# First four heads of a fused attention and mixer kernel: the scores made a second time with the keys on the partitions

## The chip, the cores and the metric

The kernel runs on one core of a Trainium2 chip. The metric is the device time of one execution in microseconds (us); the time of the kernel before is the median of three runs.

The core's engines run beside each other, each with its own queue of instructions, and wait for each other by semaphores. TensorE (PE) multiplies and writes to PSUM; VectorE (DVE) and ScalarE (ACT) read and write PSUM and SBUF; GpSimd (POOL) works on SBUF; SyncE (SP) issues the DMA transfers.

## The reference

```
scores = (q @ k^T) / 8, positions of later blocks of 64 masked      # per batch (8) and head (8), 576 x 576
attn   = exp(scores - max(scores)); attn /= sum(attn) + 1e-9
x      = attn @ v, heads side by side                               # (8, 576, 512)
theta  = x @ w_theta
y      = w_tok_r @ (x cos theta) + w_tok_i @ (x sin theta)          # over the 576 positions
u      = x + y
out    = u + max(u @ w_ch, 0)
```

q, k and v are standard normal times 0.1, q and k times some 5.8 on top. All is f32. A position sees its own block of 64 and all earlier blocks.

## The kernel before

The work goes by batch (8) and, within a batch, by pairs of heads (4). A pair's two heads (hh = 0, 1) lie on the two halves of the 128 partitions, so products of 64 rows for both run beside each other. Positions are cut into four tiles of 128 queries (i = 0 to 3, positions 64 to 575) and a tile 4, the first 64 positions of both heads in one.

For a pair, `scores_wide` (tiles 3 and 2) and `scores_narrow` (tiles 1 and 0) make q k^T with the queries on the partitions (line 610), and `mask` (line 617) adds a huge negative number to the forbidden blocks. For a head, `maxima` (line 658, VectorE) takes the maximum of each row, `bias` (lines 668 and 670) turns it into the bias of the exponential, and `exponentials` (line 674, ScalarE) writes exp to SBUF (`t`). The products with v need the keys on the partitions, so exp has to be turned. For the first eight heads TensorE turns it (`turn_up`, line 699, in 128x128 f32 tiles into PSUM) and ScalarE or VectorE copies it to SBUF (`turned_high`, lines 451 and 453); for later heads a DMA turns it. For heads 0 to 3 (`WIDE_HEADS`) all stays f32 and `weighted` (line 732) multiplies with the raw v, which has a column of ones for the sum of the row. Later heads work with pairs of f16 numbers. `normalise` divides.

In batches 0 to 2 scores use the raw f32 q and k. The weights come as wide numbers and are unpacked in steps (`Weight`: load, exponent, lowest, narrow, plain, high and low part); this fills the first 60 us of ScalarE, VectorE and GpSimd. The mixer of a batch then has theta (line 898), sines, their products with x, the mixing over positions (line 974), and the channel products (line 997).

The order of the work is written out. `add` names each part, what it needs, which PSUM banks it takes and gives back, and on which engines it may run. `ORDER` lists the 3453 parts in the order in which they are issued, `BANKS` the PSUM banks, `PLACES` the engine of each part that has a choice. So each engine's queue follows from three tables. Sixteen parts `fill` (line 1270) are two products of ones each, whose results nobody reads.

Of the kernel before, what the change touches and what calls it, by code (L numbers as in the profile page):

```python
# [12 lines left out]
F32 = mybir.dt.float32  # L13
# [21 lines left out]
HALVED = 8  # L35
# [222 lines left out]
def attention_phase_mixer(  # L258
# [40 lines left out]
    def pieces(n):  # L299
        return ("A", "B") if n < 2 * HALVED else ("all",)  # L300
# [1022 lines left out]
```

## Time and profile before

| | |
|---|---|
| median of 3 runs | 641.83 us (641.12 to 641.84) |
| the profiled execution's own time | 642.9 us |
| its span, first to last instruction | 641.1 us |
| TensorE busy | 624.5 us, 97% |
| VectorE busy | 565.0 us, 88% |
| ScalarE busy | 525.0 us, 82% |
| GpSimd busy | 349.5 us, 55% |
| mean granted TensorE clock | 0.995 |

The span is one execution, as the profiler saw it. Busy time is the time in which an engine had an instruction in work. A TensorE instruction's duration is longer than the distance to the next one, since products follow each other in a pipeline; the cost of products is therefore read from start to start, as the timeline gives it. The granted clock is the share of 2.4 GHz that TensorE got.

### The profile page before, as it was taken

The page shows a single profiled execution, that of the slowest core. Times are in us where ns is not written, and L with a number is a line of the kernel's source. Part 1 is how long each engine was busy: PE and PEld are TensorE (multiplying, and loading weights), DVE is VectorE, ACT ScalarE, POOL GpSimd, SP SyncE. Part 2 cuts the span into 40 slices and gives each one's busy share as a digit, 9 for nine tenths or more (in the row PEclk, how much of TensorE's full clock was granted, in tenths as well). Part 3 has the DMA queues.
Part 4 walks back from the last instruction along what each step waited for, and adds up shares of the span by engine and source line. Part 5 has one row for each costly group of instructions (what it writes and reads, how often), then busy time and mean ns, then how long its engine had stood idle before and what let it go on. Part 6 is the DMA issues. An engine that isn't in the chain of part 4 may idle for free.

```text
span 641.1 us, 18144 instructions
## 1 busy us (share of the span) xinstructions
PE 624.5 (97%) x7457; PEld 469.1 (73%) x7457; DVE 565.0 (88%) x1111; ACT 525.0 (82%) x886; POOL 349.5 (55%) x387
## 2 busy tenths in 40 slices
PE   7999999999999999999999999999998999999997
PEld 4788667766876688867778678775876678857775
DVE  4999999999999999999999999999999998855564
ACT  5989999889897999989998999899998987346012
POOL 4545557523626654545775567672565478744230
PEclk9899999999999999999999999999999999999999
DMA  8973998998797799977869978969797757930102
GB/s 327 384 263 86 200 214 181 190 181 194 185 237 162 157 136 223 176 172 202 172 166 219 224 138 184 218 142 229 160 200 147 124 76 154 167 74 2 38 38 75
DMA packets 238627, 109.28 MB, mean 170 GB/s; under 512 B 225360, under 2 KB 226384, under 8 KB 238544
## 3 DMA queue, kind: packets, MB, share of 16 engines
q1 hardware_dynamic: 238544, 108.12, 76.3%
q8 instruction: 58, 0.95, 0.6%
q14 instruction: 25, 0.20, 0.1%
HBM read 42.21 MB, written 9.44 MB: 81 GB/s over the span
## 4 chain that ended last, share of the span: by engine, by line
PE 51%; ACT 16%; DVE 8%; DMA 7%; issue 3%; POOL 1%; POOLq 0%; DVEq 0%; ACTq 0%
PE g L974 12%; PE s L974 9%; PE g L997 7%; PE g L741 7%; DMA pt<-p 7%; ACT t L674 5%; PE s L997 4%; PE g L898 4%; PE s L898 3%; PE s L610 3%; ACT aa L941 2%; DVE p L456 2%; DVE m L658 2%; ACT rr L939 2%; ACT junk L860 2%
## 5 line engine op out<-in xcount | busy, mean ns | idle before, releaser
L974 PEld LDWEIGHTS <-zh 128*128 128x128 f16 x1152 | 112.7, 98 | 29.7 <-issue 0.4
L974 PE MATMUL g<-wT_h,zh 128*128 128x288 f16 x351 | 100.5, 286 | 0.8 <-ACT t L674 0.8
L974 PE MATMUL g<-wT_h,zl 128*128 128x288 f16 x351 | 100.4, 286 | 0.0
L974 PE MATMUL g<-wT_l,zh 128*128 128x288 f16 x351 | 100.4, 286 | 0.0
L741 PEld LDWEIGHTS <-pt 128*128 128x128 f16 x2700 | 89.1, 98 | 7.8 <-DMA pt<-p 3.2
L741 PE MATMUL g<-v,pt 128*128 128x65 f16 x2700 | 92.6, 193 | 2.1 <-DMA pt<-p 1.6
L658 DVE TENSOR_REDUCE m<-s 128x1 f32<-128x576 f32 (+3 forms) x132 | 84.9, 671 | 2.8 <-PE s L617 2.5
L456 POOL TENSOR_TENSOR p<-t,p 128x1536 f16<-128x1536 f32 (+4 forms) x22 | 55.8, 2542 | 50.5 <-ACT p L451 35.4
L456 DVE TENSOR_TENSOR p<-t,p 128x1600 f16<-128x1600 f32 (+4 forms) x42 | 72.1, 1717 | 4.9 <-ACT p L451 4.5
L451 ACT CAST p<-t 128x1536 f16<-128x1536 f32 (+4 forms) x50 | 68.1, 1363 | 3.4 <-DMA pt<-p 2.7
L974 PEld LDWEIGHTS <-zl 128*128 128x128 f16 x576 | 56.4, 98 | 15.8 <-issue 1.2
L898 PEld LDWEIGHTS <-xT 128*128 128x128 f16 x384 | 36.6, 98 | 42.6 <-issue 1.7
L974 PE MATMUL s<-wT_h,zh 128*128 128x288 f16 x225 | 64.3, 286 | 0.0
L974 PE MATMUL s<-wT_l,zh 128*128 128x288 f16 x225 | 64.3, 286 | 0.0
L974 PE MATMUL s<-wT_h,zl 128*128 128x288 f16 x225 | 64.3, 286 | 0.0
L674 ACT ACTIVATE t<-s,m,size 128x576 f32<-128x576 f32 (+1 forms) x80 | 59.7, 779 | 4.1 <-POOL m L670 2.4
L950 POOL TENSOR_TENSOR aa<-aa,xn 128x256 f32<-128x256 f32 (+1 forms) x59 | 42.3, 728 | 35.0 <-ACT aa L941 25.9
L658 DVE TENSOR_REDUCE m<-g 128x1 f32<-128x192 f32 (+2 forms) x156 | 53.8, 369 | 6.8 <-PE g L617 6.7
L997 PEld LDWEIGHTS <-wch_h 128*128 128x128 f16 x512 | 48.3, 98 | 13.4 <-issue 1.7
L456 POOL TENSOR_TENSOR xp<-xn,xp 128x640 f16<-128x640 f32 x22 | 33.6, 1529 | 33.5 <-ACT xp L451 24.8
L674 ACT ACTIVATE t<-g,m,size 128x320 f32<-128x320 f32 (+2 forms) x100 | 50.1, 534 | 1.3 <-POOL m L670 1.0
L997 PE MATMUL g<-uh,wch_h 128*128 128x288 f16 x176 | 50.4, 286 | 0.2 <-DVE xT L1013 0.2
(209 smaller groups left out, 1659.3 us busy)
## 6 DMA issues: line engine op xcount, KB each, us to landing
rv<-in_v SPq DMA_DIRECT2D x16, 780.0 KB, 5.9
rq<-in_q SPq DMA_DIRECT2D x15, 640.0 KB, 5.2
rk<-in_k SPq DMA_DIRECT2D x15, 576.0 KB, 4.8
out<-xT SPq DMA_DIRECT2D x28, 288.0 KB, 2.8
w_raw<-in_w_tok SPq DMA_DIRECT2D x5, 576.0 KB, 8.4
pt<-in_w_tok SPq DMA_DIRECT2D x4, 576.0 KB, 9.2
w_raw<-in_w_theta SPq DMA_DIRECT2D x4, 512.0 KB, 8.1
w_raw<-in_w_ch SPq DMA_DIRECT2D x4, 512.0 KB, 5.8
```

What stands on the lines that cost most here:

```text
L451: nc.scalar.copy(out=out, in_=x)
L456: engine_of(on).tensor_tensor(out=out, in0=x, in1=y, op=ALU.subtract)
L610: nc.tensor.matmul(to[hh][:, col:col + n], lhsT=qq[rows, P + P * i:P + P * i + P], rhs=kk[rows, k0:k0 + n], start=nn == 0 and col % 512 == ...
L658: nc.vector.tensor_reduce(out=self.m[:, i:i + 1], in_=self.scores_of(i), axis=AX.X, op=ALU.max)
L674: nc.scalar.activation(out=t_parts[self.hh][:, to:to + n], in_=self.scores_of(i), func=AF.Exp, scale=self.scales()[0], bias=self.m[:, NI + ...
L741: nc.tensor.matmul(o[:, i, :], lhsT=source[:, block, :], rhs=vv[:, slot, hh, :], start=first, stop=last)
L860: nc.scalar.activation(out=to, in_=x, func=AF.Abs, accum_out=self.scales_of(what, g).sum_of(what, g))
L898: nc.tensor.matmul(g, lhsT=xT[:, xx + i, :], rhs=ww[:, dt, :], start=first, stop=last)
L939: nc.scalar.activation(out=to, in_=x, func=AF.Sin, scale=2.0 * math.pi)
L950: engine_of(on).tensor_tensor(out=cd, in0=cd, in1=self.xns[dt][:, i0:i0 + ni, :], op=ALU.mult)
L974: nc.tensor.matmul(g, lhsT=zz[:, kk, cols], rhs=ww[:, kk, ts], start=(n == 0 and kk == k0 and nn == 0), stop=n == 4 and kk == k0 + ni - 1 ...
L997: nc.tensor.matmul(g[:, 0:HS], lhsT=ww[:, dt, e * P:(e + 1) * P], rhs=uu[:, dt, th * HS:(th + 1) * HS], start=dt == 0 and n == 0, stop=dt ...
```

## The change

For heads 0 to 3 exponentials, turns and copies are replaced. The scores with the queries on the partitions are made as before, but for their maxima alone. The maximum of each row is split into three bf16 parts (`less_upper`, two subtractions for a head). A product with a bf16 identity turns the parts of all tiles into 15 rows (`maxima_turned`), which a copy takes to SBUF (`maxima_row`). Then `scores_turned` makes the scores with keys and queries exchanged, in three banks for each head (sx, sy, sz): f32 products over full blocks, half blocks of 64 output rows in the bank sz, a bf16 product for the mask of the diagonal blocks, and bf16 products of a prepared matrix of minus ones with the rows of the maxima, which subtract the maximum of each query. `first_turned` does it for the first 64 positions. ScalarE's exponential goes from there into the tile that `weighted` reads (`exponentials_turned`), in the order of `TURNED_BLOCKS`; a head's products with v are one part now where they were two. The bias steps of these heads go. The identity, the minus ones and the rows lie in the room of `p_parts[1]`, which is used by later heads only, and are prepared at the start by VectorE and GpSimd.

The three tables are new as a whole: 3441 parts, in another order throughout. The 16 fills remain. On SP's queue the loads of pair 1's q and k stand behind three weight tiles where they stood behind four. In TensorE's queue the beginning is now:

```
before: s2.0 s1.0 sd.0 tp.1.B tp.0.B s2.1 tp.0.A fill tp.1.A fill wa.0 tp.0.4 wa.1 sd.1 wa.2 wa.3 s1.1 fill vm.0 weighted.0.A ...
after:  s2.0 s1.0 sd.0 s2.1 sd.1 fill mt.0 fill mt.1 s4.0 sx.0 sy.0 sz.0 fill wa.0 wa.1 wa.2 wa.3 s1.1 weighted.0 fill mt.3 wa.4 mt.2 fill vm.0 s4.1 sx.1 sz.1 wa.5 weighted.1 sy.1 ...
```

Here s1, s2 and sd are the scores of a pair, tp the turns of a head, wa a sum over weights, mt the turn of a head's maxima, and s4, sx, sy and sz the second scores of a pair. The core of the diff, without the tables:

```diff
+    TURNED_BLOCKS = [[(0, 1), (10, 0)], [(1, 1), (4, 2), (10, 5)], [(2, 1), (5, 2), (8, 3), (11, 0)],
+                     [(3, 1), (6, 2), (9, 3), (7, 4), (11, 5)], [(12, 0)]]
+    FULL = {"sx": [(1, 0, 4, 0)], "sy": [(2, 1, 3, 0), (4, 3, 1, 384)], "sz": [(3, 2, 2, 0)]}
+    HALF = {"sx": [], "sy": [], "sz": [(0, 0, 256), (1, 1, 256), (2, 0, 384), (3, 1, 384)]}
+    DIAGONAL = {"sx": [0], "sy": [0, 384], "sz": [0]}
+    MOST = {"sx": [0, 1, 2, 3], "sy": [1, 2, 3, 3], "sz": [2, 3, 5, 6]}
...
+    early = p_parts[1].rearrange("p a c -> p (a c)").bitcast(BF16)
+    ident_b = early[:, 0:P]
+    nc.vector.tensor_copy(out=ident_b, in_=made_ident)
+    one_of = const.tile([P, NI], F32, name="one_of")
+    for row in (0, 64):
+        nc.vector.tensor_reduce(out=one_of[row:row + 64], in_=ident[row:row + 64, row:row + 3 * NI].rearrange("p (s i) -> p i s", i=NI),
+                                axis=AX.X, op=ALU.add)
+    minus = early[:, P:P * (NI + 3)].rearrange("p (a c) -> p a c", c=P)
+    nc.vector.tensor_scalar(out=minus[:, 0:NI], in0=one_of.unsqueeze(2).broadcast_to([P, NI, P]), scalar1=-1.0, scalar2=None, op0=ALU.mult)
+    for i in range(2):
+        nc.gpsimd.tensor_copy(out=minus[:, NI + i, 0:D], in_=minus[:, 2 * i, 0:D])
+        nc.gpsimd.tensor_copy(out=minus[:, NI + i, D:P], in_=minus[:, 2 * i + 1, 0:D])
+    m_split = [const.tile([P, 3, NI], F32, name=f"m3{n}") for n in range(4)]
+    m_rows = [early[:, P * (NI + 3 + n):P * (NI + 4 + n)] for n in range(2)]
+    for part in m_split + m_rows:
+        nc.gpsimd.memset(part, 0.0)
...
+        def scores_turned(self, x):
+            qq, kk = self.raw("q"), self.raw("k")
+            to = [bank_of[x, self.p, hh] for hh in range(2)]
+            both = [(hh, slice(hh * D, hh * D + D)) for hh in range(2)]
+            for slot, i, n, col in FULL[x]:
+                for hh, rows in both:
+                    nc.tensor.matmul(to[hh][:, col:col + n * P], lhsT=kk[rows, P * slot - D:P * slot + D], rhs=qq[rows, P + P * i:P + P * (i + n)],
+                                     start=col == 0, stop=False, tile_position=(hh * D, 0))
+            for i, half, col in HALF[x]:
+                for hh, rows in both:
+                    nc.tensor.matmul(to[hh][half * D:half * D + D, col:col + P], lhsT=kk[rows, 0:D], rhs=qq[rows, P + P * i:P + P * i + P],
+                                     start=False, stop=False, tile_position=(hh * D, half * D))
+            for col in DIAGONAL[x]:
+                for hh, rows in both:
+                    nc.tensor.matmul(to[hh][D:P, col:col + D], lhsT=ones[rows, 0:D], rhs=mask_q[rows, 0:D], start=False, stop=False,
+                                     tile_position=(hh * D, D))
+            for n, i in enumerate(MOST[x]):
+                for hh, rows in both:
+                    nc.tensor.matmul(to[hh][:, n * P:n * P + P], lhsT=minus[rows, i, :], rhs=m_rows[self.p % 2][rows], start=False, stop=n == 3,
+                                     tile_position=(hh * D, 0))
+
+        def first_turned(self):
+            to = bank_of["t4", 2 * self.p][0:D, 0:P]
+            nc.tensor.matmul(to, lhsT=self.raw("k")[:, 0:D], rhs=self.raw("q")[:, 0:P], start=True, stop=False)
+            nc.tensor.matmul(to, lhsT=minus[0:D, NI - 1, 0:D], rhs=m_rows[self.p % 2][0:D], start=False, stop=True, tile_position=(0, 0))
...
+        def less_upper(self, step, on):
+            x = m_split[self.n % 4]
+            less(on, x[:, step + 1, :], x[:, step, :], self.uppers()[:, step * NI:step * NI + NI])
+
+        def maxima_turned(self):
+            to = bank_of["sx", self.pair.p, self.hh][self.hh * D:self.hh * D + 3 * NI, 0:P]
+            nc.tensor.matmul(to, lhsT=self.uppers(), rhs=ident_b, start=True, stop=True)
+
+        def maxima_row(self, on):
+            rows = slice(self.hh * D, self.hh * D + 3 * NI)
+            copied(on, m_rows[self.pair.p % 2][rows], bank_of["sx", self.pair.p, self.hh][rows, 0:P])
+
+        def exponentials_turned(self, x):
+            if x == "t4":
+                to, src, rows = wide_of(self.turned)[0:D, 12, :], bank_of[x, self.n][0:D, 0:P], slice(0, D)
+            else:
+                at_ = 4 * ("sx", "sy", "sz").index(x)
+                to, rows = wide_of(self.turned)[:, at_:at_ + 4, :], slice(0, P)
+                src = bank_of[x, self.pair.p, self.hh].rearrange("p (a c) -> p a c", c=P)
+            nc.scalar.activation(out=to, in_=src, func=AF.Exp, scale=QK_SCALE, bias=lift[rows, 0:1])
...
+                if turned_early:
+                    for step in range(2):
+                        add(("ms", n, step), step_of(h.less_upper, step), [("ms", n, 0)] if step else [("m", n, i) for i in tiles], on="PD")
+                    add(("mt", n), h.maxima_turned, [("ms", n, 1)], takes=[("sx", p, hh)])
+                    add(("mc", n), h.maxima_row, [("mt", n)] + row_free, on="DA")
+                    for x in ("sx", "sy", "sz") + ("t4",) * (hh == 0):
+                        add(("ex", n, x), step_of(h.exponentials_turned, x), [("s4" if x == "t4" else x, p)] + w_free,
+                            leaves=[(x, n) if x == "t4" else (x, p, hh)])
+                    add(("weighted", n, piece), step_of(h.weighted, piece), turned_of(n, piece) + turned_of(heads[0], piece) + [("vo", pr // PG)] + o_free)
+                    continue
```

## Rows read from the trace of the kernel before

**Rows 1.** The page, part 1: busy us, share, instructions of each engine.
```profile
PE 624.5 (97%) x7457; PEld 469.1 (73%) x7457; DVE 565.0 (88%) x1111; ACT 525.0 (82%) x886; POOL 349.5 (55%) x387
```

**Rows 2.** Windows: length, busy us of each engine (instructions), clock, DMA share, GB/s.
```profile
13.60:98.30 84.70, 82.94 (x866) 62.34 (x866) 79.17 (x179) 79.57 (x145) 47.13 (x61) 0.96 0.83 235
103.40:530.00 426.60, 419.63 (x5435) 314.17 (x5432) 404.73 (x785) 391.68 (x646) 243.20 (x239) 1.00 0.87 178
530.00:641.10 111.10, 107.26 (x1036) 82.96 (x1031) 69.23 (x126) 42.26 (x75) 50.54 (x49) 1.00 0.33 76
```

**Rows 3.** Waits of TensorE: who waited for whom, us in total, times, longest.
```profile
PE g L699 <- ACT t L674: 1.9, 1, 1.9
...
PE g L610 <- DMA rq<-in_q: 1.1, 1, 1.1
...
PE g L638 <- ACT t L674: 1.0, 2, 0.8
```

**Rows 4.** Windows of 1 us at the start; the number behind POOL is the granted clock.
```profile
12.00:13.00 1.00, 0.56 (x6) 0.32 (x3) 1.00 (x4) 1.00 (x3) 0.91 (x2) 0.92 1.04 423
13.00:14.00 1.00, 0.36 (x2) 0.39 (x4) 1.00 (x2) 1.00 (x3) 0.59 (x1) 0.50 1.04 427
...
19.00:20.00 1.00, 1.00 (x8) 0.99 (x7) 0.79 (x3) 1.00 (x2) 0.00 (x0) 0.66 0.97 399
```

**Rows 5.** Windows, with the fills' line alone, over the whole span.
```profile
0.00:641.10 641.10, 9.18 (x32) 2.88 (x32) 0.99 0.77 170
```

**Rows 6.** Timeline of TensorE, turns: start, us, line, operands, count [idle before].
```profile
18.48 1.63 PE L699 MATMUL s<-ident_r,t 128*128 128x128 f32 x8
...
57.11 1.04 PE L699 MATMUL s<-ident_r,t 128*128 128x128 f32 x8
57.98 1.52 PE L741 MATMUL g<-v,pt 128*128 128x65 f16 x45
```

**Rows 7.** Timeline of TensorE, 39.2 to 41.5 us: a pair's wide scores and mask.
```profile
39.25 2.17 PE L610 MATMUL s<-rk,rq 64*128 64x512 f32 x16
41.25 0.22 PE L617 MATMUL s<-ones,mask_q 64*128 64x128 bf16 x2
41.40 0.77 PE L699 MATMUL g<-ident_r,t 128*128 128x128 f32 x5
```

**Rows 8.** Timeline of TensorE, theta's last rows in two column halves.
```profile
85.34 0.41 PE L901 MATMUL g<-wth_h,xT 128*64 128x256 f16 x4
85.59 0.28 PE L901 MATMUL g<-wth_l,xT 128*64 128x256 f16 x2
```

**Rows 9.** Timeline of TensorE, narrow f16 scores of a later pair, and its mask.
```profile
309.64 0.84 PE L610 MATMUL g<-qk 64*128 64x320 f16 x18
310.31 0.22 PE L617 MATMUL g<-ones,mask_q 64*128 64x128 bf16 x2
```

**Rows 10.** Groups, 0 to 43.3 us: line, operation, shapes, count, busy us, mean ns, idle before.
```profile
L674 ACT ACTIVATE t<-s,m 128x576 f32<-128x576 f32 (+1 forms) x8 | 5.3, 696 | 0.4 <-POOL m L670 0.4
...
L674 ACT ACTIVATE t<-g,m 128x320 f32<-128x320 f32 (+2 forms) x12 | 4.8, 441 | 0.1
...
L453 DVE COPY pt<-s 128x1024 f32<-128x1024 f32 (+1 forms) x3 | 2.6, 905 | 0.4 <-ACT junk L860 0.4
...
L451 ACT COPY pt<-s 128x1024 f32<-128x1024 f32 x2 | 2.0, 1004 | 0.0
...
L451 ACT COPY pt<-g 128x512 f32<-128x512 f32 (+1 forms) x3 | 1.4, 478 | 0.0
L453 DVE COPY pt<-g 128x512 f32<-128x512 f32 x2 | 1.4, 680 | 0.0
...
L497 ACT ACTIVATE w_raw<-w_raw,eighth 128x576 int32<-128x576 uint8 x1 | 0.8, 835 | 0.0
...
L501 DVE TENSOR_SCALAR w_raw<-w_raw 128x576 uint32<-128x576 uint32 x1 | 0.5, 453 | 0.0
```

**Rows 11.** Timeline of VectorE, its first maxima and the wait before them.
```profile
7.21 0.89 DVE L658 TENSOR_REDUCE m<-g 128x1 f32<-128x320 f32 x2 [4.74 <-PE g L617]
```

More of the change, by code (lines that the diff above doesn't have):

```diff
@@ L223 @@
+    "1235401235401235401234601235401234601234601234501235401235601235601234601235601236501234601236401236501236524654"
+    "0651445650546624654130143066645166605051431066645545056616026345051046561046656405340414405544416542015464160645"
+    "5646464100451345323640256314365612053040412045362400310266664645546"
 )
 PLACES = (
[L225 to L226 removed]
@@ new lines @@
+    "PAPASADAPADDAPADAPADAPADAAAAPDAPPPADDDPDADAAADAAADDPAADDADAAPDDAAPAPASAAAPADDADADDAPDPAADAAPADAAAAAPADASPAPDAAAP"
+    "ADPAAPDPDAADPDADADAAPAAAADAADAAAADAAAAAAADDSPAPDSAAAPADAAPAPDDAAPPDDDAPPPAAAAAPADAAPDDDPAAADADDSDAPDPAAAPDPASDAD"
+    "DPAAAAAPDAAAPAPPPADDDAAAADAAPPAPAPAPDAADDPDAPDPAPDPPPDDDDDPPDPDADDDAPDPAPDPAPPPDPPADPPADAAAAADDAAADAPDPAPDDDADDD"
+    "PPDPAPDDPPPDAPDPADDPADPPADPPDDPPADPPADDADADDPAAAAAADAAPDPDAPPPAAADADDADPDAPDPPPPPPPPDAPDPAPDDAPPDAPPPPDPPAPPDDAP"
+    "PPAAAAADDADAPADPPADDDDADPPAPDPAPDPAPDPPPPPAPDPAPDPAPDPAPPDADPPADPPDADPPADAAAAADDAPPPADAPAAAAAPPAPDPPPDPAPPDADPPP"
@@ L235 @@
+    "PPPAPPPAPDPAPDDAPDPADPAPAPPPADDAADAADADADPDAPDADDDPPPDDPAPDPADPPAPDDADPPAPPPADDDAPPDPPPPPPDDDAPADAAAADDAAAADAPAP"
+    "PDDDDDAPDPDDPPPPPAPPDAPPPPDPPDPDPDDPDAPPPPDPDPPPDDDPADPAAAAAAADADADPPADDDDADPDDDPDADDPAPDDPDDDADPPPDDPDPDPDDDPAD"
+    "DPDDPAPAPDPPAAADADAA"
 )
@@ L299, in pieces @@
     def pieces(n):
-        return ("A", "B") if n < 2 * HALVED else ("all",)
+        return ("A", "B") if WIDE_HEADS <= n < 2 * HALVED else ("all",)
     def extent(hh, piece):
@@ L656, in maxima, with uppers @@
             if not hasattr(self, "m"):
-                self.m = at.tile([P, 10], F32, tag="m", name="m", bufs=4)
+                self.m = m_split[self.n % 4][:, 0, :] if self.n < WIDE_HEADS else at.tile([P, 10], F32, tag="m", name="m", bufs=4)
             nc.vector.tensor_reduce(out=self.m[:, i:i + 1], in_=self.scores_of(i), axis=AX.X, op=ALU.max)
+        def uppers(self):
+            return m_split[self.n % 4].rearrange("p a c -> p (a c)").bitcast(BF16).rearrange("p (c two) -> p c two", two=2)[:, :, 1]
+        def less_upper(self, step, on):
[15 more added lines that the diff above has]
+            nc.scalar.activation(out=to, in_=src, func=AF.Exp, scale=QK_SCALE, bias=lift[rows, 0:1])
         def scales(self):
@@ L705, in turned_parts @@
             x = self.turned_in(piece)[:, 0:n * P].rearrange("p (a c) -> p a c", c=P)
-            if self.n < WIDE_HEADS:
-                at_ = {"A": 4, "B": 0, "4": 12}[piece]
-                return x, wide_of(self.turned)[:, at_:at_ + n, :], None
             return (x,) + tuple(self.turned[:, at_ + y:at_ + y + n, :] for y in (0, room // P))
@@ L730, in weighted @@
                 if self.n < WIDE_HEADS:
+                    blocks, rows = TURNED_BLOCKS[i], slice(0, P if i < 4 else D)
                     for j, (at_, slot) in enumerate(blocks):
-                        nc.tensor.matmul(o[:, i, :], lhsT=wide_of(source)[:, at_, :], rhs=pair.raw("v")[:, slot, hh, :],
+                        nc.tensor.matmul(o[:, i, :], lhsT=wide_of(source)[rows, at_, :], rhs=pair.raw("v")[rows, slot, hh, :],
                                          start=j == 0, stop=j == len(blocks) - 1)
@@ L1081, in attention_phase_mixer @@
     mixers = [Mixer(b) for b in range(B)]
+    again = ["sx", "sy", "sz", "s4"]
     for b, m in enumerate(mixers):
@@ L1088, in attention_phase_mixer @@
                         for n in ({"q": ["ql"], "k": ["kl"], "v": ["v2"]} if b >= WHOLE else
-                                  {"q": ["s1", "s2", "sd"], "k": ["s1", "s2", "sd"], "v": ["v2"]})[what] if what != "v" or 2 * p >= WIDE_HEADS]
+                                  {"q": ["s1", "s2", "sd"] + again * (2 * p < WIDE_HEADS), "k": ["s1", "s2", "sd"] + again * (2 * p < WIDE_HEADS), "v": ["v2"]})[what] if what != "v" or 2 * p >= WIDE_HEADS]
                 if what == "v":
@@ L1123, in keys, with early_done @@
         return [(name, n, x) for x in pieces(n)]
+    def early_done(n):
+        return [(x, p) for p in range(WIDE_HEADS // 2) for x in again] if n == WIDE_HEADS + 1 else []
     for p in range(B * NPAIR):
@@ L1145, in attention_phase_mixer @@
         add(("s2", p), pair.scores_narrow, ready, takes=[("s2", p, hh) for hh in range(2)])
-        add(("sd", p), pair.scores_first, ready + turn_of("first", [("e", heads[0], 4)], 2))
+        add(("sd", p), pair.scores_first, ready + turn_of("first", [("me"[heads[0] >= WIDE_HEADS], heads[0], 4)], 2))
+        if 2 * p < WIDE_HEADS:
+            row_free = turn_of("m_row", [(x, p) for x in again], 2)
+            known = [("mc", n) for n in heads]
+            for x in again:
+                add((x, p), step_of(pair.scores_turned, x) if x != "s4" else pair.first_turned, ready + (known if x != "s4" else known[:1]),
+                    takes=[("t4", heads[0])] if x == "s4" else [(x, p, hh) for hh in range(2)] if x != "sx" else ())
         for hh, n in enumerate(heads):
@@ L1150, in attention_phase_mixer @@
             e_all = [("e", n, i) for i in tiles]
-            free_m = turn_of("m", e_all, 4)
+            turned_early = n < WIDE_HEADS
+            free_m = turn_of("m3", [("mt", n)], 4) if turned_early else turn_of("m", e_all, 4)
             for i in tiles:
-                add(("m", n, i), step_of(h.maxima, i), [("sd" if i == 4 else "s1" if i > 1 else "s2", p)] + free_m)
+                gone_with = {3: [("s1", p, hh, 0), ("s1", p, hh, 1)], 2: [("s1", p, hh, 1)], 4: []}.get(i, [("s2", p, hh)])
+                add(("m", n, i), step_of(h.maxima, i), [("sd" if i == 4 else "s1" if i > 1 else "s2", p)] + free_m,
+                    leaves=gone_with if turned_early else ())
             w_free, o_free = turn_of(f"pt{hh}", [x for m_ in (heads if hh == 0 else [n]) for x in keys("weighted", m_)], 2), turn_of("o", [("normalise", n, 2)])
@@ L1160, in gone @@
                 return [(name, n, x) for x in pieces(n) if "all" in (x, piece) or x == piece]
-            def t_last(n):
-                return "th" if n < WIDE_HEADS else "tl"
             def turned_of(n, piece):
+                if n < WIDE_HEADS:
+                    return [("ex", n, x) for x in ("sx", "sy", "sz")] + [("ex", n, "t4") for _ in range(n % 2 == 0)]
                 if n < PE_TURNED:
-                    return [(t_last(n), n, piece)] + [(t_last(n), n, "4") for _ in range(piece == "A" and n % 2 == 0)]
+                    return [("tl", n, piece)] + [("tl", n, "4") for _ in range(piece == "A" and n % 2 == 0)]
                 return [("turn", n, piece)]
             for piece in pieces(n):
+                if turned_early:
[8 more added lines that the diff above has]
+                    continue
                 mine = [i for i in tiles if i in TILES[piece]]
@@ L1186, in attention_phase_mixer @@
                         leaves = {"A": [("s1", p, hh, k) for k in range(2)], "B": [("s2", p, hh)], "4": [("t4", n)]}[x]
-                        add(("th", n, x), step_of(h.turned_high, x), [("tp", n, x)] + w_free, leaves=leaves if n < WIDE_HEADS else (), on="AD")
-                        if n >= WIDE_HEADS:
-                            add(("tl", n, x), step_of(h.turned_low, x), [("th", n, x)], leaves=leaves)
+                        add(("th", n, x), step_of(h.turned_high, x), [("tp", n, x)] + w_free, on="AD")
+                        add(("tl", n, x), step_of(h.turned_low, x), [("th", n, x)], leaves=leaves)
                 else:
                     same = gone(n - 2, piece, "turn")
-                    add(("high", n, piece), step_of(h.high, piece), [("e", n, i) for i in mine] + same, on="ADP")
+                    add(("high", n, piece), step_of(h.high, piece), [("e", n, i) for i in mine] + same + early_done(n), on="ADP")
                     add(("low", n, piece), step_of(h.low, piece), [("high", n, piece)], on="PD" if piece == "B" else "DP")
```

17 lines of the change are left out of this document (3 added, 14 removed), and 347 rows, old and new, of the table ORDER.

## The prediction

> **What bounds the kernel now.** I read the page first, then the busy time by stage, then TensorE's waits, then single stretches of the timeline. The page says that TensorE is busy for 97% of the span, more than any other engine [rows 1]. The reader is to see in the table by stage where the other 3% lie [rows 2]. In 13.6 to 98.3 us, in which the changed work stands, TensorE is busy for 82.94 of 84.70 us, so it waits 1.8 us there in all; VectorE and ScalarE are busy for 79.2 and 79.6 us of the same stretch. All three are nearly full, but TensorE is the fullest. From 103.4 to 530 us TensorE idles 7.0 us of 426.6 while the two others idle 22 and 35 us. After 530 us they idle for 38% and 62%, and TensorE for 3.8 us of 111.1. So the end is set by the sum of TensorE's work plus its own idle time, and a microsecond more of work on it is one more at the end unless an idle one goes.
>
> Three parts of TensorE's time are not work. The waits [rows 3]: 1.9 us for the first exponentials and 1.1 us for the second pair's q, both before 13.7 us; a later one, for exponentials, is 0.8 us. The clock [rows 4]: granted 1.00 (2.4 GHz), then 0.50 (1.2 GHz) from the end of the 13th microsecond to within the 20th, behind that first wait; 0.92 of one row and 0.66 of another put its ends at 12.84 and 19.68 us, and 6.8 us at half speed lose 3.4 us. The fills [rows 5]: 32 products of ones, 9.2 us, in 16 parts; they remain.
>
> **The change, TensorE.** For heads 0 to 3 it removes 50 turns of 128x128 f32 tiles (12 for each head, one more for the first rows of each pair). Eight of them took 0.87 us, from 57.11 to 57.98 [rows 6], so 50 cost 5.45 us.
>
> It adds, for each of two pairs, both heads of a pair beside each other on the two halves of the rows:
> - The scores once more in f32. The wide scores have 1024 columns and took 2.00 us, from 39.25 to 41.25 [rows 7]: 1.95 ns a column. The new ones have 512 + 512 + 256 columns over all 128 output rows, and four times 128 over 64 output rows. If two of these four run beside each other it is 1536 columns, 3.0 us; if not, 1792, 3.5 us. No row has f32 products of 64x64; nearest are theta's last rows, whose two column halves of 256 go beside each other: four in 0.25 us, from 85.34 to 85.59 [rows 8], 0.06 each, where 256 columns of f16 over the whole width take 0.11 by the columns of [rows 9]. I take 3.0 us.
> - 12 bf16 products of 128 columns, which subtract the maximum, and 4 of 64 columns, the mask. From below: the later f16 scores make 1536 columns for both heads in 0.67 us, from 309.64 to 310.31 [rows 9], 0.056 us for 128; that gives 0.8 us. From above: the mask pair together with the change of the array's shape behind it, 0.15 us (41.25 to 41.40 [rows 7]); that gives 2.4 us for 16. I take 0.8 plus six changes of shape (128 output rows to 64 and back, in each of three banks) at 0.15 - 0.056, some 0.09: 1.35 us.
> - The first rows: 128 columns at 1.95 ns and one bf16 product, 0.4 us (0.3 to 0.45). The two turns of the maxima: 0.25 us (0.1 to 0.3).
>
> One pair: 3.0 + 1.35 + 0.4 + 0.25 = 5.0 us; two: 10.0 us (8.4 to 13.3). The f32 products with v stay at 15 for each head. Net on TensorE: 10.0 - 5.45 = +4.55 us (3.0 to 7.9).
>
> **ScalarE and VectorE.** Five copies out of PSUM go from each: 2.0 + 1.4 = 3.4 us from ScalarE, 2.6 + 1.4 = 4.0 us from VectorE [rows 10]. A head's exponentials have the same 1536 columns in three instructions for four: 12 of 0.70 us (the mean of 576 and 448) for 8 of 0.70 and 8 of 0.44 [rows 10], 0.7 us less. VectorE gets four copies of a maxima row (128 columns, some 0.3 each by the larger copies) and two of eight subtractions of five columns. Sum: ScalarE -4.1 us, VectorE -2.5 us. Of the unpacking of weights three steps go to ScalarE (0.84 each) and four to VectorE (0.45 each) [rows 10], away from GpSimd: what is left is -1.6 and -0.7 us. I cost this at no gain, since TensorE covers it. GpSimd has six subtractions for six biases. The constants prepared at the start (on VectorE a copy of 128 columns, two small sums and one product of 640 columns) lie in VectorE's wait of 4.7 us before 7.2 us [rows 11]; without that cover they would cost about 2 us once.
>
> **The new waits.** A head's maximum over all its columns has now to be known before its first exponential. The chain is: last maximum, two subtractions, a turn on TensorE, a copy on VectorE, the second scores. Behind that turn in TensorE's queue stand a fill and then the second scores themselves, so TensorE waits. For pair 0 this takes the place of the 1.9 us wait, and pair 1's scores and two fills stand in it; pair 1's q and k are issued one weight tile sooner on SP's queue. I put it at zero (-1 to +1.5). For pair 1, whose turns come behind the first head's products with v, I take 0.5 us (0 to 1.5). Behind the copies on VectorE's queue stand weight conversions, whose users come later; behind ScalarE's first new exponential stand more unpackings, which I count as part of pair 0's bound.
>
> **What is given back.** A TensorE that comes later finds its feeders further ahead. Of its 7.0 us of idle time from 103.4 to 530 us [rows 2] I take a quarter, 1.8 us (0 to 5), since VectorE and ScalarE in turn wait for TensorE. The new tables move nearly every part by some places and 380 parts to another engine; I give that no sign, and 1.5 us either way.
>
> **The clock.** The slow stretch began behind the first wait, and it ended within eight turns (18.48 us on [rows 4, 6]); turns and products are mixed in it. In the sum it stays 6.8 us long. The Trainium skill ("TensorE: Matmul & The Clock Gate", Part 4: PE-mode transpose) says that a transpose doesn't count as activity of TensorE as a product does; by that, products in place of turns would bring the clock back sooner, and no row here shows or excludes it.
>
> **The sum.** The profiled execution's own time was 642.9 us (span 641.1), 1.1 us over the median of 641.83; I add the difference to the median. 641.8 + 4.55 + 0.5 - 1.8 = 645.1 us.
>
> **Rivals.**
> 1. No difference. Either the whole delay of 5 us is given back, for which 7.0 us of idle time are enough, or the slow stretch goes because products keep TensorE at 2.4 GHz where turns and a wait stood: 645.1 - 3.4 = 641.7 us. For: the idle time is there, and pair 1's scores come sooner into the first gap. Against: the first gap stays as long as maxima are outstanding, and the feeders wait for TensorE themselves.
> 2. Faster: ScalarE and VectorE are the pace of 13.6 to 98 us, and TensorE only looks full because of fills, behind which it still waits 0.8 us for an exponential at 98 us [rows 3]. Then what is taken from them comes off: 0.7 to 1.6 us with the unpacking they get, 2.5 to 4.1 us if that finds idle time; 637.7 to 641.1 us, 639.4 in the middle. It decides where TensorE's waits in the stretch, without fills, exceed the 4.55 us added. For: 9.2 us of fills, and both engines over 93% busy [rows 2]. Against: the fills are still in the order and cost their time, and only 1.8 us of waiting can be won.
> 3. Much slower: the round trip for pair 1's maxima leaves TensorE idle a second time, and the clock falls there too for another 6.8 us: +3.4 us, 648.5 us. For: one wait of 2 us sufficed at the start. Against: pair 1 has the first products with v and the weights' sums to go between.
>
> That the change isn't what it says (still turning, or copying) is excluded by the code: the exponentials of these heads write the turned tiles directly.
>
> **How the numbers follow.** Forecast, 643.1 to 647.5 us: 0.50. Rival 1: 0.22. Rival 2: 0.16. Rival 3 and other losses above 647.5: 0.12. About 0.2% (1.3 us) can be told from no change here, so slower has 0.62, same 0.22, faster 0.16. The range reaches from below the middle of rival 2 to past rival 3, and to the ends of the unknown costs: 641.8 + 3.0 - 1.0 - 5 is 638.8 at the least, and 641.8 + 7.9 + 0.5 - 1.8 is 648.4; so 638.8 to 649.0 us. The likeliest case alone: 643.1 to 647.5.
>
> **What would show it.** In the profile after: turns halved to 50, no f32 copies into the turned tiles, twelve exponentials of 512 columns; about 5 us of TensorE for each pair's second scores; the first mixing product some 4 us later than 103.4 us; TensorE's idle time from there to 530 us some 2 us lower. It would be wrong if TensorE's busy time didn't grow by about 4 us, if the first mixing product came no later, or if the granted clock never fell.

## The result and the profile after

The changed kernel took 649.56 us (median of four executions: 647.28, 649.12, 650.00, 650.61), the kernel before 641.48 us (640.97 to 641.84). The ratio is 1.0122, 95% interval 1.0093 to 1.0151: slower by 8.1 us by the medians, 7.8 us by the ratio, where 645.1 was forecast and 649.0 was the end of the range. In the order of these times the executions' mean granted clocks were 0.999, 0.995, 0.997 and 0.995. The profiled execution is the fastest, and that of the kernel before (642.9 us) is slower than its median, so the two traces lie only 4.4 us apart (645.5 against 641.1 us of span).

The page's busy times of the changed kernel, in answer to [rows 1]:

```profile
PE 627.4 (97%) x7545; PEld 470.0 (73%) x7545; DVE 565.9 (88%) x1128; ACT 522.8 (81%) x889; POOL 344.9 (53%) x369
```

The windows that answer to [rows 2], the first to the end of the wait ahead of heads 6 and 7's products with v (before, to the end of a wait ahead of a pair's first scores), then from the first mixing product, which comes at 108.33 us (before, 103.37 us):

```profile
13.60:101.40 87.80, 82.57 (x895) 60.07 (x894) 83.59 (x183) 76.98 (x139) 40.16 (x53) 1.00 0.78 224
108.30:530.00 421.70, 415.29 (x5354) 311.58 (x5351) 391.62 (x771) 390.66 (x657) 245.22 (x221) 1.00 0.86 179
530.00:645.50 115.50, 111.77 (x1116) 86.39 (x1113) 76.64 (x140) 43.28 (x76) 51.40 (x47) 1.00 0.38 80
```

In the first stretch TensorE idles for 5.2 of 87.8 us; it was 1.8 of 84.7. From the first mixing product to the end it is 537.2 us, and 537.7 before: next to nothing is given back. In the first stretch, which is 3.1 us longer, GpSimd has 7 us less to do (47.1 to 40.2) and VectorE 4.4 more. From the start to the first mixing product, before and after, VectorE (the third number pair) does 6.7 us more, where the forecast had 0.7 us less:

```profile
0.00:103.37 103.37, 97.60 (x998) 71.97 (x999) 91.02 (x202) 91.08 (x167) 55.74 (x100) 0.97 0.81 239
0.00:108.33 108.33, 100.36 (x1085) 72.09 (x1086) 97.71 (x219) 88.84 (x158) 48.31 (x102) 1.00 0.76 228
```

The start, in answer to [rows 4]: the clock stays at 1.00 in this execution.

```profile
12.00:13.00 1.00, 1.00 (x15) 0.79 (x12) 1.00 (x2) 0.51 (x1) 0.36 (x2) 1.00 1.01 415
13.00:14.00 1.00, 1.00 (x5) 0.20 (x3) 0.80 (x5) 0.89 (x3) 0.62 (x2) 1.00 1.02 420
...
19.00:20.00 1.00, 1.00 (x13) 0.43 (x6) 1.00 (x3) 0.80 (x2) 0.61 (x1) 1.00 0.97 388
```

TensorE's timeline: the second scores of pair 0 begin at 14.16 us, and the next part, a fill, follows at 19.10; those of pair 1 begin at 28.09 us.

```profile
14.16 0.43 PE L679 MATMUL s<-rq,rk 128*64 128x128 f32 x2
...
19.10 0.60 PE L1360 MATMUL s<-ones 128*128 128x512 bf16 x2
...
28.09 0.43 PE L679 MATMUL s<-rq,rk 128*64 128x128 f32 x2
...
30.64 0.32 PE L666 MATMUL s<-rq,rk 64*64 64x128 f32 x1
30.65 0.32 PE L666 MATMUL g<-rq,rk 64*64 64x128 f32 x1
30.66 0.32 PE L666 MATMUL s<-rq,rk 64*64 64x128 f32 x1
30.66 0.32 PE L666 MATMUL g<-rq,rk 64*64 64x128 f32 x1
30.80 0.27 PE L666 MATMUL s<-rq,rk 64*64 64x128 f32 x1
```

Pair 0's take 4.94 us where 5.0 was forecast. This work is as foreseen; TensorE's waits from 13 to 110 us are not (who waited for whom, us in total, times, longest; on TensorE L770 is the turns, L810 the products with v, L685 a pair's first scores, L535 the sums of weights; L745 is the exponentials, L729 the new ones, L832 and L838 the division by the sums):

```profile
PE s L770 <- ACT t L745: 1.6, 1, 1.6
PE g L810 <- ACT t L745: 1.5, 1, 1.5
PE g L810 <- DVE xn L838: 0.7, 1, 0.7
PE g L685 <- DVE r L832: 0.6, 1, 0.6
PE g L770 <- ACT t L745: 0.4, 1, 0.4
PE s L535 <- ACT pt L729: 0.3, 1, 0.3
```

The longest follows from a chain that timelines of four engines show. Pair 2's wide scores, at 39.25 us before [rows 7], now come at 48.78 us, behind the products with v of heads 2 and 3; only then VectorE can take the four maxima, GpSimd the bias and ScalarE the exponentials, and TensorE stands still until the turns:

```profile
48.78 0.69 PE L631 MATMUL s<-rk,rq 64*128 64x512 f32 x1
...
51.37 2.48 DVE L705 TENSOR_REDUCE m<-s 128x1 f32<-128x448 f32 x4
...
52.81 0.19 POOL L741 TENSOR_SCALAR m<-m 128x3 f32<-128x3 f32 x1 [4.80 <-DVE m L705]
...
53.04 1.90 ACT L745 ACTIVATE t<-s,m 128x576 f32<-128x576 f32 x3 [2.24 <-POOL m L741]
...
54.36 0.87 PE L770 MATMUL s<-ident_r,t 128*128 128x128 f32 x6 [1.58 <-ACT t L745]
```

By stage, the kernel before and the changed one (columns as in [rows 2]); before:

```profile
13.00:45.00 32.00, 31.09 (x235) 25.10 (x235) 28.77 (x63) 29.03 (x54) 16.21 (x22) 0.90 0.88 339
45.00:75.00 30.00, 29.31 (x371) 23.48 (x370) 27.92 (x70) 28.55 (x55) 17.61 (x27) 1.00 0.59 152
75.00:108.00 33.00, 32.24 (x381) 22.26 (x380) 32.37 (x71) 32.26 (x59) 20.61 (x23) 1.00 0.97 185
```

and after:

```profile
13.00:45.00 32.00, 31.70 (x313) 23.28 (x311) 29.03 (x72) 28.16 (x50) 8.12 (x15) 1.00 0.86 331
45.00:75.00 30.00, 26.54 (x346) 22.07 (x343) 28.75 (x59) 24.87 (x50) 14.65 (x21) 1.00 0.46 138
75.00:108.00 33.00, 31.49 (x362) 20.84 (x360) 31.95 (x73) 31.12 (x56) 21.14 (x23) 1.00 0.89 177
```

TensorE's idle time from 45 to 108 us is 5.0 us (3.46 + 1.51) against 1.4 (0.69 + 0.76).

Another view is the chain of work that ended last, followed back from the end by the profile (start, us, what). In the kernel before it can be followed to 80 us; from there to 127 us it is on TensorE for 2.7 us only, and otherwise on ScalarE, VectorE, GpSimd and the DMA turns of later heads:

```profile
81.51 1.55 ACT t L674 x4
...
110.07 8.82 DMA pt<-p
```

In the changed kernel it isn't on TensorE at all from 80 to 125 us:

```profile
80.50 1.94 DVE m L705 x3
...
101.29 2.41 ACT t L745 x4
...
109.71 1.33 DVE m L705 x3
...
115.55 8.37 DMA pt<-p
```

The links of such a chain are inferred, so this supports a pace set by the other engines there and doesn't prove it.

### The profile page after: what moved, and what is told of

Same layout as the page of the kernel before. It is cut to its first block, busy times and chain, and to the rows that moved or that the text cites. A ratio compares the mean times of both kernels' runs of the same rounds, so it can differ in the third digit from the quotient of the medians.

```text
span 645.5 us, 18326 instructions
## 1 busy us (share of the span) xinstructions
PE 627.4 (97%) x7545; PEld 470.0 (73%) x7545; DVE 565.9 (88%) x1128; ACT 522.8 (81%) x889; POOL 344.9 (53%) x369
## 4 chain that ended last, share of the span: by engine, by line
PE 57%; ACT 23%; DVE 7%; DMA 5%; issue 4%; POOL 2%; SPq 0%; DVEq 0%; ACTq 0%
PE g L1043 13%; PE s L1043 8%; ACT t L745 7%; PE g L810 6%; PE g L1066 6%; PE g L967 6%; PE s L967 6%; PE s L631 4%; PE s L1066 3%; ACT p L472 3%; DMA pt<-p 2%; ACT junk L929 2%; ACT aa L1010 2%; PE g L631 2%; DVE m L705 1%
## 5 line engine op out<-in xcount | busy, mean ns | idle before, releaser
L810 PE MATMUL g<-v,pt 128*128 128x65 f16 x2700 | 92.3, 193 | 4.3 <-ACT t L745 2.0
L810 PEld LDWEIGHTS <-pt 128*128 128x128 f16 x2700 | 89.4, 97 | 9.5 <-issue 3.7
L477 POOL TENSOR_TENSOR p<-t,p 128x1536 f16<-128x1536 f32 (+3 forms) x23 | 62.3, 2709 | 53.9 <-ACT p L472 38.3
L705 DVE TENSOR_REDUCE m<-s 128x1 f32<-128x448 f32 (+2 forms) x134 | 85.9, 669 | 2.7 <-PE s L638 2.5
L477 DVE TENSOR_TENSOR p<-t,p 128x1600 f16<-128x1600 f32 (+4 forms) x41 | 69.3, 1690 | 5.4 <-ACT p L472 4.9
L472 ACT CAST p<-t 128x1536 f16<-128x1536 f32 (+4 forms) x47 | 63.8, 1360 | 2.2 <-DMA pt<-p 1.5
L745 ACT ACTIVATE t<-s,m,size 128x576 f32<-128x576 f32 (+1 forms) x80 | 59.9, 782 | 4.1 <-POOL m L741 2.5
L1019 POOL TENSOR_TENSOR aa<-aa,xn 128x256 f32<-128x256 f32 (+1 forms) x59 | 46.5, 800 | 21.6 <-ACT aa L1010 21.2
L477 POOL TENSOR_TENSOR zl<-aa,zh 128x512 f16<-128x512 f32 (+1 forms) x29 | 36.1, 1252 | 35.4 <-ACT zh L472 30.3
L745 ACT ACTIVATE t<-g,m,size 128x320 f32<-128x320 f32 (+2 forms) x100 | 49.9, 539 | 4.0 <-POOL m L741 2.8
```

Of the source, the lines that this page charges most:

```text
L472: nc.scalar.copy(out=out, in_=x)
L477: engine_of(on).tensor_tensor(out=out, in0=x, in1=y, op=ALU.subtract)
L705: nc.vector.tensor_reduce(out=self.m[:, i:i + 1], in_=self.scores_of(i), axis=AX.X, op=ALU.max)
L745: nc.scalar.activation(out=t_parts[self.hh][:, to:to + n], in_=self.scores_of(i), func=AF.Exp, scale=self.scales()[0], bias=self.m[:, NI + ...
L810: nc.tensor.matmul(o[:, i, :], lhsT=source[:, block, :], rhs=vv[:, slot, hh, :], start=first, stop=last)
L1019: engine_of(on).tensor_tensor(out=cd, in0=cd, in1=self.xns[dt][:, i0:i0 + ni, :], op=ALU.mult)
```

## Experiments

Times are medians, differences go by the ratio to the kernel before that was run beside it (1% is 6.4 us). The number in brackets behind a ratio is its 95% interval. The changed kernel stands at 1.0122 (1.0093 to 1.0151), so a difference of 1 to 2 us from it lies within the intervals. A feeder of TensorE is here whatever makes its operands: the unpacking of weights, maxima, exponentials and copies.

### What TensorE's work is worth in the kernel before

More work, no new wait:

```
-        for _ in range(2):
+        for _ in range(9 if n in (2, 3, 4) else 2):
```

> The kernel before with nine products of ones instead of two in the fills 2, 3 and 4: 21 more bf16 products of 512 columns, about 4.5 us of TensorE's work by the other fills, in the stretch in which the change adds its 4.55 us, with no new wait, no new order and no new bank. Theory A (the end is the sum of TensorE's work, next to nothing is given back later): 641.5 + 4.5 = 646.0 us. Theory B (the prediction's: a quarter of the idle time after 103.4 us, 1.8 us, is given back): 644.2 us. Theory C (ScalarE and VectorE are the pace there and TensorE only looks full): 641.5 to 642.5 us. If it is A, what the change costs above 4.6 us is waits of its own; if it is near 649, a delay at this place grows behind it and the new waits aren't needed.

646.27 us, ratio 1.0083 (1.0064 to 1.0102): +5.3 us (4.1 to 6.5) for some 4.5 us of work. By the medians this is theory A, and theory B's 644.2 us lies outside the interval; but the six executions spread from 643.8 to 647.8 us, and the profiled one (645.15) reaches the first mixing product at 105.86 us, only 2.5 us later than the kernel before. TensorE was full from 45 to 75 us (29.95 of 30).

Less work, first all fills (`range(0)`), then fills 5 and 6 alone:

> The kernel before without its 32 products of ones (9.2 us of TensorE). Theory A (sum of TensorE's work): the fills that stand where TensorE doesn't wait come off the end; at least the some 4 us of those before 74 us, so 637 us or less, unless the granted clock falls a second time. Theory C (ScalarE and VectorE are the pace): TensorE only waits where it filled before, 641.5 us. The granted clock by stretch is to be read beside it: a second stretch at half speed would show what the fills are for.

643.91 us, 1.0046 (1.0034 to 1.0058): slower, by neither theory. Without fills TensorE stood still for 1.7 us (to 29.49 us) and 2.7 us (to 98.04 us) where fills had been, and at each of the two the clock fell. At a third wait, of 1.8 us, it stayed at 1.00:

```profile
93.84 1.51 PE L741 MATMUL g<-v,pt 128*128 128x65 f16 x45 [1.83 <-DVE xn L769]
```

Windows of this kernel, the clock is the number behind POOL:

```profile
28.00:32.00 4.00, 2.51 (x12) 2.52 (x13) 3.59 (x10) 4.00 (x8) 3.35 (x4) 0.69 1.03 410
...
100.00:104.00 4.00, 4.00 (x22) 2.50 (x22) 2.32 (x4) 3.54 (x8) 2.74 (x4) 0.50 0.55 104
```

> The kernel before without fills 5 and 6 (four products of ones at 48 to 50 us, 0.9 us). Without any fills TensorE had no wait there. If TensorE's work sets the end there: 0.9 us less than before, 640.6 us, which would beat both kernels; if a feeder is right behind it: 641.5 us.

641.41 us, 1.0000 (0.9992 to 1.0009). The 0.9 us don't come off. Why is not shown: in the profiled execution TensorE is busy for 29.86 of the 30 us from 45 to 75, so no feeder makes it wait where the fills were. So 4.5 us added at 24 to 32 us cost their time by the medians, and 0.9 us removed at 48 to 50 us win nothing; the same place wasn't tried with both signs.

### The clock

Products of ones in the first gaps, of the kernel before (8 and 4) and of the changed one (7):

```
+            if self.p == 0:
+                keep_busy(8, 5)
```

> The kernel before with 8 products of ones behind the first scores' maxima and 4 behind the first turns, so that TensorE doesn't stand still between 9.5 and 13.6 us. If the idle time there is why the clock falls to half for 6.8 us: no stretch at 0.50 in the profile, and 641.5 - 3.4 = 638.1 us. If the clock falls for another reason, or the products delay the path: 641.5 us or above.

642.56 us, 1.0029 (1.0012 to 1.0045). In the profiled execution (643.58 us, mean clock 0.993) the clock held until 25 us, but TensorE, being earlier, now waited for weights and exponentials from 16 to 25 us, and behind that the clock fell after all (windows below). Eight of the twelve executions had a mean clock of 0.999 or 1.000, and they took 640.6 to 643.8 us: 3.4 us of clock weren't there to be won. The kernel before says the same: its two executions at 1.000 took 640.31 and 640.43 us, 0.6 and 1.3 us less than the medians of the runs they belong to.

```profile
22.00:25.00 3.00, 1.12 (x12) 0.55 (x10) 1.53 (x4) 2.66 (x5) 2.37 (x4) 1.00 0.98 395
25.00:30.00 5.00, 5.00 (x27) 4.38 (x27) 4.99 (x12) 4.58 (x9) 2.91 (x5) 0.57 0.83 273
```

> The changed kernel with 7 products of ones behind its first scores. In its profiled execution the clock never fell and it took 647.3 us; its other executions had lower mean clocks (0.995 to 0.997) and took 649.1 to 650.6. If it is the first gap of TensorE that decides between these, all executions come at a mean clock of 0.999 and at about 647 us, and the difference from the kernel before is 5.8 us and not 8.1. If not: 649 to 650 us, as without the products.

648.22 us, 1.0119 (1.0104 to 1.0135). Three executions at a mean clock of 1.000 took 647.7 to 648.6 us, so at full clock the loss is still some 6 to 7.5 us (the changed kernel's execution at 0.999 took 647.28). The fourth, profiled one, at 0.997, took 650.50 us, and its clock didn't fall at the start: it was 1.00 up to 345 us and fell behind a wait there.

```profile
347.73 0.19 PE L689 MATMUL g<-qk 128*128 128x64 f16 x1 [2.36 <-DVE qk L612]
...
349.00:350.00 1.00, 1.00 (x14) 0.50 1.27 290
```

The changed kernel's trace has a wait of 1.18 us at this place, and the clock stays at 1.00. So a mean clock of 0.995 to 0.997 doesn't tell that the slow stretch of the start was there; where it lay in the changed kernel's slower executions (649.1 to 650.6 us) isn't known.

### The second scores' work in the changed kernel

```
-  nc.tensor.matmul(to[hh][:, col:col + n * P], lhsT=kk[rows, ...], rhs=qq[rows, ...], ...)
+  nc.tensor.matmul(to[hh][:, col:col + n * P], lhsT=minus[rows, 0, :], rhs=ones[rows].unsqueeze(1).broadcast_to([D, n, P]), ...)
```

> The changed kernel with the f32 products of the second scores (heads 0 to 3) replaced by bf16 products of constants of the same shapes, so that these heads' exponentials aren't those of the scores; order, banks, waits and everything else as in the changed kernel. By the fills a bf16 product of 512 columns takes 0.22 us where the f32 one takes about 1.0, so TensorE has 2 x (3.0 - 0.65) = 4.7 us less. Theory S (the sum of TensorE's work sets the end): 4 to 5 us less than the changed kernel, 644 to 645 us, and the new waits stay. Rival F (ScalarE and VectorE are the pace): the waits grow by what is taken, and less than 2 us is won.

646.61 us, 1.0085 (1.0068 to 1.0101): 2.4 us less by the ratios, 2.9 by the medians, of 4.7 us of work. Between the two expectations. In the profiled execution the rest turned into waits for the feeders ahead of 45 us (28.65 of 32 us busy, at a mean clock of 0.96; 31.70 at 1.00 in the changed kernel), two of which are

```profile
PE g L535 <- DVE wth_h L542: 1.4, 1, 1.4
PE s L535 <- ACT pt L729: 1.1, 1, 1.1
```

(L535 sums the weights for their scale), while its waits after 45 us stayed as they were:

```profile
45.00:75.00 30.00, 26.53 (x320) 22.19 (x320) 28.04 (x60) 25.85 (x50) 14.51 (x20) 1.00 0.52 145
75.00:108.00 33.00, 31.49 (x364) 20.68 (x363) 31.93 (x72) 30.20 (x54) 20.45 (x25) 1.00 0.91 183
```

### The waits after 45 us

Pair 2's wide scores earlier (14 parts moved, six tiles in other banks; `EARLIER` is a list of (part, behind which)):

```
+    for key, behind in EARLIER:
+        order.remove(key)
+        order.insert(order.index(behind) + 1, key)
```

> The changed kernel with the third pair's wide scores put ahead of the first head-2 products with v on TensorE (they stood some ten microseconds later), their maxima, biases and exponentials put earlier in the same way, the exponentials that free PSUM banks 0, 2 and 5 put ahead of others on ScalarE, and six tiles given other banks. No work is added or removed. Theory W (the new waits of TensorE, 1.6 and 0.4 us at 54 and 58 us and those behind them, come from these late scores): no wait of TensorE near 54 us, 1.5 to 3 us less than the changed kernel's 648 to 649.6, so 646 to 647 us. Rival F (ScalarE and VectorE have too much to do there in the new tables, whatever the order): the wait comes back at another place and the time stays within 1 us.

652.01 us, 1.0167 (1.0144 to 1.0190): slower. The wait of 1.58 us is gone, but from 45 to 75 us there are now six waits of 0.25 to 0.83 us, for exponentials, copies, sums and divisions, where there were four; TensorE is busy for 25.86 of the 30 us from 45 to 75 (26.54 in the changed kernel). Theory W, that the late scores are the cause, has fallen.

> Both edits together: earlier scores of the third pair, and the second scores of heads 0 to 3 as bf16 products of constants (so not those heads' scores). If the changed kernel's loss is the second scores' work plus the waits for the late scores, the two gains add: 6 to 8 us less than the changed kernel, 641 to 643 us, about the kernel before. If they overlap, no more than the larger of the two.

649.71 us, 1.0115 (1.0097 to 1.0134): 1.9 us more than with the cheap products alone, within the intervals. The earlier scores win nothing here either, and the gains don't add.

VectorE lighter, with no step moved:

```
-  nc.vector.tensor_reduce(..., in_=self.scores_of(i), ...)
+  nc.vector.tensor_reduce(..., in_=self.scores_of(i)[:, 0:64] if 4 <= self.n < 8 else self.scores_of(i), ...)
```

> The changed kernel, with the maxima of heads 4 to 7 taken over the first 64 columns of each instruction's scores only, not over all of them (and the factor that keeps exponentials large 2^5 instead of 2^15 for that): 16 of VectorE's instructions take some 0.22 us instead of 0.35 to 0.75, about 5 us less of VectorE ahead of 65 us; order, engines, banks and TensorE's work are unchanged. Theory V (VectorE is the pace of 45 to 75 us in the changed kernel): TensorE's waits there shrink from 3.5 us to under 1.5, and it takes 645 to 647 us. Rival O (the waits are a chain behind late scores, VectorE's load doesn't matter): less than 1 us is won.

648.20 us, 1.0099 (1.0085 to 1.0113): 1.5 us less, which is within the intervals and between the two expectations. TensorE's idle time from 45 to 75 us falls from 3.46 to 2.38 us, with VectorE busy for only 25.73 us:

```profile
45.00:75.00 30.00, 27.62 (x352) 22.59 (x350) 25.73 (x60) 25.94 (x51) 15.48 (x22) 1.00 0.49 144
```

> The kernel before with the same shortened maxima of heads 4 to 7. TensorE waits for 0.7 us from 45 to 75 us there. Theory S (before is bounded by TensorE's work): at most 0.7 us is won, 641 us. If VectorE were the pace before as well: 638 to 639 us.

640.13 us, 0.9976 (0.9967 to 0.9985): 1.5 us less here too, again between the two expectations. A lighter VectorE helps both kernels by about the same, so the full maxima of heads 4 to 7 don't explain the difference between them. Whether the 6.7 us more that VectorE has in the changed kernel do isn't answered by this, as they remain in it.

> The changed kernel with the shortened maxima and with the second scores of heads 0 to 3 as bf16 products of constants (4.7 us less of TensorE). Alone the constants won 2 to 3 us. Theory V: with VectorE lighter, TensorE's 4.7 us can come off as well, 641 to 643 us. Rival O: 645 to 646.6 us.

644.97 us, 1.0046 (1.0032 to 1.0060). Just below rival O's range, so theory V has no support. With the second scores' products cheap TensorE's work is about level with the kernel before (4.55 - 4.7 us by the forecast's sum, an estimate). Still 0.70% or 4.5 us (some 3.4 to 5.6 by the two intervals) stand between this kernel and the kernel before with the same short maxima. The cheap products themselves are worth 0.53% or 3.4 us here.

> The changed kernel with the third pair's wide scores earlier and with the shortened maxima of heads 4 to 7 (the two edits that were tried alone). Theory B (the waits after 45 us need both causes): TensorE waits for less than 1.5 us from 45 to 75 us, and it takes 645 to 646 us. Rival O (each part of the order waits for its own chain): the waits stay above 2.5 us and it takes about 1.6 us less than with the earlier scores alone, 650 us.

647.80 us, 1.0087 (1.0072 to 1.0103). Neither expectation: 2.95 us of waiting stayed from 45 to 75 us (theory B wanted under 1.5), yet the time is 2 us under rival O's. It is no better than the short maxima alone to within the intervals, so no gain of the earlier scores shows even with a lighter VectorE.

### The tables

Parts put on the engines that the other kernel's tables give them, order and banks left alone:

```
             place[key] = next(places, parts[key].on[0])
+    place.update(ELSEWHERE)
```

> The changed kernel, with the 55 steps ahead of the first mixing product that the new tables gave to another engine, and that the kernel before has too, back on the engine of before (17 from VectorE and 10 from ScalarE to GpSimd, 9 and 10 the other way, 9 between ScalarE and VectorE); order and banks as in the changed kernel. Up to the first mixing product GpSimd is 7 us less busy in the changed kernel than before, VectorE 6.9 us more. Theory V (VectorE and ScalarE, loaded by the new tables, are the pace from 32 to 75 us, and TensorE's new waits of about 5 us are theirs): those waits shrink and it takes 645 to 647 us against 648 to 649.6. Rival O (the order and the longer way through the second scores make the waits, whichever engine does a step): within 1 us of the changed kernel, or slower, since GpSimd takes about twice as long for a step.

659.71 us, 1.0288 (1.0260 to 1.0315).

> The changed kernel with only the 17 steps that went from GpSimd to VectorE ahead of the first mixing product back on GpSimd (about 7 us less for VectorE by 98 us). Theory V: 645 to 647 us, nearly all of what the 55 steps give. Rival O: within 1 us of the changed kernel or slower.

654.94 us, 1.0209 (1.0184 to 1.0235). Both are much slower, as rival O's "or slower" has it: the new order counts on the new engines. Theory V fell in the form in which I had put it; that the old engines are slower in this order doesn't show what the new ones cost in it.

> The kernel before with the 53 steps ahead of its first mixing product that the change moves to another engine put there, and nothing else of the change: no second scores, order and banks of before. Theory V: VectorE is fuller here too and new waits of TensorE come up, 643 to 645 us against 641.5. Rival O: 641 to 642 us.

649.88 us, 1.0135 (1.0121 to 1.0150): the new engines alone, in the old order and without any second scores, cost 8.7 us. Both expectations were far too small. VectorE is busy for 97.2 us up to the first mixing product, so its 6 us more come with the moved steps and not with the second scores. TensorE idles for 7.5 us from 13 to 108 us instead of 2.4 (at full clock nearly throughout), spread over more than ten waits:

```profile
13.00:45.00 32.00, 28.91 (x227) 22.15 (x225) 30.58 (x69) 28.66 (x53) 10.94 (x15) 0.96 0.85 323
45.00:75.00 30.00, 27.73 (x346) 22.47 (x346) 27.78 (x66) 26.41 (x54) 14.54 (x22) 1.00 0.58 145
75.00:108.00 33.00, 30.90 (x353) 20.33 (x352) 32.22 (x66) 29.77 (x52) 16.28 (x18) 1.00 0.88 174
...
0.00:108.77 108.77, 97.78 (x997) 70.97 (x998) 97.24 (x210) 91.89 (x168) 45.93 (x87) 0.98 0.78 226
```

So each order is slower with the other's engines: 8.7 us in the old order, 1.7% or some 11 us in the new one (1.0288 against 1.0122). Neither number is the price of the tables as they were changed, order and engines together.

## Why the prediction was wrong

**The sign and the work.** Slower was the likeliest sign, and TensorE's added work was sized well: 4.94 us for pair 0's second scores against 5.0. That four f32 products of 64x64 run beside each other held (the groups of four start 0.11 to 0.16 us apart).

**"The sum of TensorE's work plus its own idle time": half right.** In the kernel before 4.5 us more cost 5.3 by the medians, but 0.9 us less won nothing. In the changed kernel 4.7 us less won 2.4 us, or 3.4 with short maxima. So here a sum of one engine's work told what added work costs and not what removed work wins, and from 80 to 125 us the chain that ended last hardly runs over TensorE in either kernel. Rival 2's remark that TensorE only looks full because of fills has this for it, though the direction it forecast was wrong: the two fills at 48 to 50 us cost nothing, and without any fills the clock fell at two more places.

**"What is given back", 1.8 us: measured about 0.5.** The time from the first mixing product to the end went from 537.7 to 537.2 us, and by the medians the added products alone gave nothing back. The first mixing product came 4.96 us later, near the forecast "some 4 us", but by luck: the forecast kept the slow stretch, and the changed kernel's trace has none. In the kernel before without fills 5 and 6, whose trace has the clock at 1.00 up to there as well, the product comes at 101.11 us; 108.33 is 7.2 us later, or 6.3 if the 0.9 us of fills are taken off.

**"The new waits", 0.5 us, and the tables, "no sign, and 1.5 us either way": the step that failed.** Ahead of 45 us, where I had put the 0.5 us, there is one new wait of 0.3. From 45 to 108 us TensorE idles 3.5 us more than before: in pairs 2 and 3, whose code the change doesn't touch. Their scores come at other places, and their steps run on other engines. With TensorE's work made about level and the maxima short in both kernels, 4.5 us of the difference remain. I had counted 380 moved parts and given them no sign without a reason. Of VectorE's load I counted only the unpackings and the second scores' own steps, which gave 0.7 us less and no cost; up to the first mixing product it has 6.7 us more, and about as much (6.2) with the new engines alone.

Put together, with short maxima in both kernels: 7.9 us of difference, of which 3.4 go when the second scores' f32 products are made cheap, and 4.5 stay (each to about 1 us either way). These 4.5 are what is left when the other is taken away: the new order, engines and banks and the longer way from the maxima to the exponentials of heads 0 to 3 are all in them, and no run separates them. "The engines" alone can't be charged with them, since each order is slower with the other's engines.

**The range.** Its upper end took TensorE's work at its worst (7.9 us) but left the waits at 0.5, the give-back at 1.8 and the tables at nothing, though the text gives them up to 3.0 (1.5 for each pair), nothing and 1.5. With those ends it would have reached to 654.2 us. The measured time lies near rival 3's 648.5 us, but its mechanism didn't come: up to 108 us of the trace the clock is 1.00, and there is no second long wait for pair 1's maxima.

**The signs.** TensorE's busy time grew by 2.9 us (624.5 to 627.4) where about 4 was asked for, its idle time from the first mixing product to 530 us fell by 0.6 us (7.0 to 6.4) and not by 2, and in the profiled execution the clock never fell, which the prediction had named as a sign of being wrong.

**The clock.** The forecast took 3.4 us for the slow stretch; the executions of the kernel before at full clock are 0.6 and 1.3 us below their medians. In the profiled execution of the changed kernel products stood where turns had been, and the clock stayed at 1.00. By the Trainium skill ("TensorE: Matmul & The Clock Gate", Part 4: PE-mode transpose) a transpose doesn't count as activity of TensorE as a product does; this trace agrees with it. But three executions of the same kernel had mean clocks of 0.995 to 0.997, and in the kernel before with products of ones the clock fell later, behind a wait. So these runs don't decide on the rule.

**Left open.** Which edge of the new order makes the waits after 45 us, and whether VectorE's 6.7 us more are the cause or go with it. Moving pair 2's scores, relieving VectorE, or both took away 1.1 us of waiting at most, and going back in engines alone made it worse; an order written for the second scores with the old engines from the start wasn't tried. That PSUM banks forced pair 2's scores back (the second scores hold up to six of eight) is read from the tables, not shown. None of the versions beat the kernel before, apart from the kernel before with part of the maxima left out.

## What to carry to other kernels

An engine at 97% with fills in its queue told here what added work costs, not what removed work wins: try both signs before summing, and look at the chain that ended last beside the busy shares. Where a change comes with order, engines and banks written anew, price the tables by themselves, in the stretch behind the edit as well, and count every engine's moved steps; here 4.5 of some 8 us were left when the added work was taken out. And a late part in the order can be a symptom: when its wait was taken away, several smaller ones came in its place.

## What was not expected of the hardware

Behind waits of 1.7 and 2.7 us the granted clock fell to 0.50 (1.2 GHz) again further into the run (some 29.5 to 33 and 98 to 104.5 us, in the kernel without fills), and once behind a wait of 2.4 us at 348 us (the changed kernel with products of ones), not only at the start; behind a wait of 1.8 us at 92 to 94 us in the kernel without fills, and behind one of 1.6 us at 54 us in the changed kernel, it stayed at 1.00. And in one execution with the first gaps filled with products, the slow stretch came at 25 us instead of 13 us: the engine that was early waited, and lost the clock there.
